# Mixture-of-experts tail on one core: another order of the expert programs, and five weight tiles subtracted on VectorE

## The chip, the core and the metric

One core of a Trainium2 chip runs the whole kernel. The metric is the device time of one execution in microseconds (us), from first to last instruction plus the little that lies around it. The median of three runs of the kernel before is 533.0 us (533.0 to 534.43). What can be told from no change with this kernel is about 0.3%, or 1.6 us.

The names of the engines are those of the profile: PE (TensorE matmuls; PEld is its weight load), DVE (VectorE), ACT (ScalarE), POOL (GpSimd), SP (SyncE, which only issues DMAs here). A "q" behind a name, as in PEldq, is the engine's sequencer: branches, register loads, semaphore waits.

## What is computed

Three stages, all in float32:

```python
x = attention(q, k, v)                 # 2 x 768 tokens, 8 heads of 64 -> x: 1536 x 512
x = elu(x @ w_in) @ w_out              # 512 -> 2048 -> 512
logits = x @ w_gate                    # 8 experts
e = argmax(logits, axis=1); gate_w = softmax(logits)[e]
# tokens go to their expert in order, at most capacity = 384 of them each
h = maximum(disp[e] @ w1[e], 0)        # 512 -> 1024
y = h @ w2[e]                          # 1024 -> 512
out[i] = gate_w[i] * y[token i]        # 0 for a token over the capacity
```

Everything that the change touches lies in the last stage, from the moment the tokens are routed.

## The kernel before

A float32 matmul is done as three passes of a faster type: each operand is split into a rounded half (`[:, 0]`, "hi") and the rest (`[:, 1]`, "lo"), and hi*hi, hi*lo and lo*hi are summed. So every 128x512 chunk of an expert's weights has to be *converted* before PE can use it: a cast from `rawq` (float32, fresh from DMA) to the hi half, mostly on ACT (L559), and a subtraction for the lo half (L560) on DVE or on POOL. That is `conv_expert(k, ms, pool, vec)`: chunks `ms` of expert `k`; those in `pool` have their subtraction on POOL, those in `vec` their cast on DVE. When a chunk is converted, its raw buffer is loaded again by SP. An expert has NCHUNK = 16 chunks, eight for w1 and eight for w2; experts of even and odd rank have tile sets `E0_*` and `E1_*`, and activation tiles `xbq0` and `xbq1`.

The experts are taken by falling number of tokens. The rank order is known only at run time, and so are the counts, so the program has branches (`tc.If`/`c.Else`, which end up as COMPARE_BRANCH on each of the five engines, after a TENSOR_LOAD of the count from `regs` in `count`, L1184). With the inputs of this case, the sorted counts are 880, 425, 168, 62, 1, 0, 0, 0. With blocks of 128 tokens and at most nj = 3 blocks for an expert, the work is:

- the first block of the largest expert (`Block`, tiles `bh0f`, `bh1f`), spread by hand over the end of the second stage and the routing of the last 384 tokens (L1069 to L1130). This part is one order written out by hand; `next(last)` runs a piece of the routing (`route`, L440 to L513) on DVE and PE, and `conv_expert(0, ...)` calls stand between the pieces;
- k = 0, the other two blocks of the same expert: `many_blocks(0, 2, ...)` (L692 `bh`, L681 `y`);
- k = 1 with three blocks, k = 2 with two blocks: `many_blocks`;
- k = 3 and k = 4 with one block: `one_block` (L618 `bh`, L626 transposes, L642 `y`). The last one has nothing to prefetch, and its names end in z (`bh_1z`).

While expert k computes, `more` converts the weights of expert k+1 in small portions and `ahead` transposes its gathered tokens (L582 `bt`); `finish` scales by the gate (L593 to L596) and scatters rows to `out` on POOL (L597).

Which code an expert runs is chosen by `blocks(k, cv, more_come)` with `choose(nb)`: is the count over 256? then three blocks; else over 128? then two; else one. Around it `experts(k, cv)` asks whether the next expert has tokens at all and puts the variant without prefetch into the Else branch, behind everything that the Then branch holds, all later experts included.

```python
                def choose(nb):
                    if k and nb == 1 and js[0] == 0:
                        body(1)
                        return
                    with tc.If(cv > js[nb - 1] * P) as c:
                        body(nb)
                    if nb > 1:
                        with c.Else():
                            choose(nb - 1)
            with tc.If(nxt > 0) as c:
                blocks(k, cv, True)
                experts(k + 1, nxt)
            with c.Else():
                blocks(k, cv, False)
```

So the program runs forward through code for three, two and one block of each expert, and jumps over what it does not need. Counted in PE's instruction list of the program (a matmul with its weight load counts as two), with these counts PE's way is: at the end of k=0 an unconditional jump of 170 instructions; end of k=1, one of 432; at k=2 a taken compare-branch of 363 (not over 256); end of k=2 an unconditional jump of 124; at k=3 taken compare-branches of 363 and 308 (not over 256, not over 128); after k=3 one of 4630 (no tokens in rank 5), then of 341 and 293 (not over 256, not over 128) to the block of k=4. The far jump is of 653 instructions on ACT, 605 on DVE, 268 on POOL and 446 on SP.

Of the kernel before, what the change touches and what calls it, by code (L numbers as in the profile page):

```python
# [20 lines left out]
P = 128  # L21
# [9 lines left out]
N = NB * S  # L31
# [10 lines left out]
NE = 8  # L42
# [4 lines left out]
GRP = 3  # L47


def build(tc, cap, qT, kT, vT, vP, wi, wo, wg, wgT, wx, out):  # L50
# [6 lines left out]
    with ctx:  # L57
# [488 lines left out]
        def raw_of(k, m):  # L546
            return RAW[m % NRAW] if k == 0 else RAW[((k - 1) * NCHUNK + m) % len(RAW)]

        def raw_load(k, ms):
            for m in ms:  # L550
                nc.sync.dma_start(raw_of(k, m), wx[ds(ereg[k], 1), :, m, :].rearrange("o p f -> p (o f)"))

        def conv_expert(k, ms, pool=(), vec=()):
            for m in ms:
                w, raw = EW[k][m], raw_of(k, m)
                if m in vec:
                    nc.vector.tensor_copy(w[:, 0], raw)
                else:
                    nc.scalar.copy(w[:, 0], raw)  # L559
                (nc.gpsimd if m in pool else nc.vector).tensor_tensor(w[:, 1], raw, w[:, 0].bitcast(F32), op=ALU.subtract)  # L560
                nxt = m + len(RAW)
                if nxt < NCHUNK:
                    raw_load(k, [nxt])
                elif 0 < k < NE - 1:
                    raw_load(k + 1, [nxt - NCHUNK])
# [8 lines left out]
        def gather(xg, gidx, n):  # L574
            nc.gpsimd.indirect_dma_start(
                out=xg, out_offset=None, in_=x2d[0:n, :],
                in_offset=bass.IndirectOffsetOnAxis(ap=gidx, axis=0))

        def load_xT(xb, col, xg, nm):
            pt = psm("bt" + nm, "TSO"[col // P])  # L580
            for c in range(NCC):
                nc.tensor.transpose(pt[:, c * P : (c + 1) * P], xg[:, c * P : (c + 1) * P], ident)  # L582
            ptv = pt.rearrange("p (c q) -> p c q", q=P)
            q = slice(col, col + P)
            nc.scalar.copy(xb[:, 0, :, q], ptv)
            nc.vector.tensor_tensor(xb[:, 1, :, q], ptv, xb[:, 0, :, q].bitcast(F32), op=ALU.subtract)
# [482 lines left out]
        next(last)  # L1069
        blk.first(0, 2)  # L1070
        blk.first(0, 3)
        conv_expert(0, range(11, 12), pool=range(NCHUNK))
        next(last)
        blk.turn(0, lo=False)
        blk.first(1, 0)
        conv_expert(0, range(12, NCHUNK), pool=range(NCHUNK))
        next(last)
        blk.turn_lo(0)
        blk.first(1, 1)
# [3 lines left out]
        blk.second(0)  # L1083
        blk.second(1)
        blk.turn(1, lo=False)
        next(last, None)
        blk.second(2)
        blk.second(3)
# [32 lines left out]

        GS = {0: slots(tf0.rearrange("p (j v) -> p j v", v=3), nj, "a") + (0,)}
        gathers(0, GRP)
        blk.turn_lo(1)
        cnt, key = count_key("1", NT)
        for f in range(4, 8):
            blk.second(f)
# [56 lines left out]
            return nc.values_load(regs[0:1, 1, k : k + 1], min_val=0, max_val=N,  # L1184
                                  skip_runtime_bounds_check_because="a count of tokens")

        def blocks(k, cv, more_come):

            jstart = 1 if k == 0 else 0
            gate, gidx, sidx, c0 = GS[k]  # L1190

            def fetch(nm, nb, pool):
                if not more_come:
                    return lambda n: None, lambda: None
                gathers(k + 1, nb)
                todo = list(range(NCHUNK))

                def more(n):
                    for m in todo[:n]:
                        conv_expert(k + 1, [m], pool, pool)  # L1200
                    del todo[:n]

                return more, lambda: ahead(k + 1, nb, nm)

            def only_fetch():
                more, ah = fetch(f"_{k}f", GRP, ())
                more(NCHUNK)
                ah()

            if k == 0 and nj == 1:  # L1210
                only_fetch()
            for j0 in range(jstart, nj, GRP):
                js = range(j0, min(nj, j0 + GRP))

                def body(nb):
                    sl = [c0 + j for j in js[:nb]]
                    nm = f"_{k}_{j0}_{nb}" + ("" if more_come else "z")
                    xb = XB[k % 2]
                    more, ah = lambda n: None, lambda: None
                    if j0 == jstart:  # L1220
                        more, ah = fetch(nm, GRP if k == 0 else nb, range(2, NCHUNK, 3) if nb == 1 else ())
                    else:
                        for i in range(nb):
                            gather(XG[i], gidx[:, sl[i] : sl[i] + 1], N)
                            load_xT(xb, i * P, XG[i], f"{i}" + nm)
                    args = (cols(gate, sl), cols(sidx, sl), nm, more, ah)
                    if nb == 1:
                        one_block(k, xb, *args)
                    else:
                        many_blocks(k, nb, xb, *args)  # L1230

                def choose(nb):
                    if k and nb == 1 and js[0] == 0:
                        body(1)
                        return
                    with tc.If(cv > js[nb - 1] * P) as c:
                        body(nb)
                    if nb > 1:
                        with c.Else():
                            choose(nb - 1)  # L1240
                    elif j0 == jstart and k == 0:
                        with c.Else():
                            only_fetch()

                choose(len(js))

        def experts(k, cv):

            if k + 1 == NE:
                blocks(k, cv, False)  # L1250
                return
            nxt = count(k + 1)
            with tc.If(nxt > 0) as c:
                blocks(k, cv, True)
                experts(k + 1, nxt)
            with c.Else():
                blocks(k, cv, False)

        experts(0, count(0))


_NAMES = ["qT", "kT", "vT", "vP", "wi", "wo", "wg", "wgT", "wx"]
# [35 lines left out]
```

## Time and profile before

| what | value |
| --- | --- |
| median of 3 runs | 533.0 us (533.0 to 534.43) |
| the profiled execution | 533.54 us, of which the span is 531.8 us |
| mean granted PE clock | 0.964 of full |
| PE busy | 482.4 us, 91% of the span |
| DVE, ACT, POOL busy | 335.8, 270.0, 202.1 us |
| chain that ended last, by engine | PE 65%, DVE 12%, DMA 8%, issue 7% |

"issue" is time in which an engine waited for nothing that the profile shows. Of the whole span PE is nearly always busy; the stretches in which it is not lie at the beginning, in the routing of the last tokens (374 to 393 us) and between the last experts (477 to 509 us).

### The profile page before, as it was taken

What the parts mean: (1) busy time and instruction counts of PE and PEld (TensorE: products, weight loads), DVE (VectorE), ACT (ScalarE), POOL (GpSimd) and SP (SyncE); (2) the same over time, 40 slices, a digit from 0 to 9 for tenths busy, and PEclk for the clock granted to TensorE, in tenths of its full rate; (3) what the DMA queues carried; (4) which work ended last, traced back from release to release, by engine and by line L of the source; (5) the groups of instructions that cost most, each with busy time, mean ns of one, the idle gap of its engine ahead of it and who ended that gap; (6) DMA issues with size and microseconds to landing.
All of it is one profiled execution on the core that took longest, in us unless ns stands there. A gap on an engine that the chain in (4) does not pass through costs nothing.

```text
span 531.8 us, 9284 instructions
## 1 busy us (share of the span) xinstructions
PE 482.4 (91%) x3052; PEld 415.0 (78%) x3052; DVE 335.8 (63%) x882; ACT 270.0 (51%) x688; POOL 202.1 (38%) x202
## 2 busy tenths in 40 slices
PE   6878888999999999999999999999889999896473
PEld 5666766878888889999999898888579898875362
DVE  4799999799888831111289888566767554563600
ACT  4656556865665456653333333337438654663310
POOL 4354756444334426862233232224650300302400
PEclk9998899999999999999999999999899999997868
DMA  8996574886666243465010100126349663764710
GB/s 235 299 244 187 167 214 122 265 253 216 181 208 178 80 127 92 120 252 164 0 61 0 60 0 2 60 65 221 112 137 337 215 219 109 219 203 130 221 35 6
DMA packets 45637, 80.01 MB, mean 150 GB/s; under 512 B 4604, under 2 KB 19196, under 8 KB 45552
## 3 DMA queue, kind: packets, MB, share of 16 engines
q1 hardware_dynamic: 43792, 73.83, 45.0%
q0 software_dynamic: 1760, 5.19, 3.2%
q8 instruction: 36, 0.59, 0.5%
q14 instruction: 49, 0.40, 0.3%
HBM read 65.29 MB, written 13.11 MB: 147 GB/s over the span
## 4 chain that ended last, share of the span: by engine, by line
PE 65%; DVE 12%; DMA 8%; issue 7%; another core or an unknown queue 3%; ACT 2%; POOL 1%; POOLq 0%; SPq 0%; DVEq 0%
PE acc L373 23%; PE h L340 22%; PE bh L692 6%; PE y L681 5%; DMA out<-ys,sidx 5%; DMA vt<-vT 3%; PE S L231 2%; PE O L279 2%; DVE t1i L319 2%; DVE t1o L322 1%; DVE t1i L322 1%; DVE st L258 1%; ACT sc L252 1%; PE T L267 1%
## 5 line engine op out<-in xcount | busy, mean ns | idle before, releaser
L340 PE MATMUL h<-xT,Wi 128*128 128x384 f32 x768 | 150.5, 345 | 8.2 <-DVE e L351 6.6
L340 PEld LDWEIGHTS h<-xT,Wi 128*128 128x128 f32 x768 | 138.3, 192 | 15.8 <-DVE e L351 8.7
L373 PE MATMUL acc<-Wo,g 128*128 128x512 f32 x576 | 146.8, 398 | 1.7 <-POOL Wo L329 1.0
L360 POOL TENSOR_TENSOR g<-e,g 128x384 fp32r<-128x384 f32 x63 | 77.2, 1225 | 123.4 <-ACT g L356 108.7
L373 PEld LDWEIGHTS acc<-Wo,g 128*128 128x128 f32 x576 | 105.4, 188 | 23.6 <-POOL Wo L329 1.3
L351 DVE SCALAR_TENSOR_TENSOR e<-e,h 128x384 f32<-128x384 f32 x64 | 35.3, 552 | 75.6 <-ACT e L347 75.6
L346 ACT ACTIVATE e<-h 128x384 f32<-128x384 f32 x64 | 31.5, 493 | 58.9 <-PE h L340 56.8
L260 POOL TENSOR_TENSOR sc<-sc,st 128x360 f32<-128x360 f32 x32 | 31.3, 979 | 67.2 <-DVE st L259 54.7
L560 DVE TENSOR_TENSOR E<-rawq,E 128x512 fp32r<-128x512 f32 x65 | 43.5, 713 | 11.9 <-ACT E L559 10.7
L252 ACT ACTIVATE sc<-sc,st 128x120 f32<-128x120 f32 x96 | 36.7, 384 | 26.4 <-DVE st L245 26.3
L356 ACT CAST g<-e 128x384 fp32r<-128x384 f32 x64 | 32.8, 512 | 33.2 <-DVE e L351 33.2
L692 PE MATMUL bh<-xbq,E 128*128 128x256 f32 (+1 forms) x288 | 43.3, 302 | 2.6 <-ACT ys L593 1.9
L692 PEld LDWEIGHTS bh<-xbq,E 128*128 128x128 f32 x288 | 41.2, 188 | 4.7 <-issue 1.7
L559 ACT CAST E<-rawq 128x512 fp32r<-128x512 f32 x75 | 42.5, 617 | 1.3 <-issue 0.7
L681 PE MATMUL y<-E,g 128*128 128x512 f32 x168 | 41.7, 393 | 0.0
L435 DVE CUSTOM_DVE_ANT_0 dot<-a,wgb 128x512 f32<-128x512 f32 x48 | 40.0, 888 | 0.0
L681 PEld LDWEIGHTS y<-E,g 128*128 128x128 f32 x168 | 30.6, 188 | 5.7
L347 ACT ACTIVATE e<-e 128x384 f32<-128x384 f32 x64 | 33.6, 526 | 2.0
L271 ACT COPY pT<-T 120x384 f32<-120x384 f32 x32 | 15.3, 478 | 37.0 <-PE T L267 36.7
L245 DVE CUSTOM_DVE_ANT_0 sc<-S,masks 128x120 f32<-128x120 f32 x96 | 22.0, 276 | 10.0 <-PE S L231 8.1
L231 PE MATMUL S<-kw,qt 64*64 64x120 f32 x384 | 27.1, 274 | 0.4 <-DVE st L245 0.3
L700 DVE TENSOR_TENSOR g<-e,g 128x256 fp32r<-128x256 f32 (+1 forms) x24 | 11.3, 471 | 25.4 <-ACT g L699 25.3
(216 smaller groups left out, 644.9 us busy)
## 6 DMA issues: line engine op xcount, KB each, us to landing
rawq<-wx SPq DMA_DIRECT2D x88, 256.0 KB, 3.8
rawi<-wi SPq DMA_DIRECT2D x16, 512.0 KB, 4.8
rawo<-wo SPq DMA_DIRECT2D x16, 512.0 KB, 4.7
vw<-vP SPq DMA_DIRECT2D x16, 288.0 KB, 6.7
kt<-kT SPq DMA_DIRECT2D x8, 400.0 KB, 5.8
qt<-qT SPq DMA_DIRECT2D x16, 192.0 KB, 4.9
vt<-vT SPq DMA_DIRECT2D x8, 384.0 KB
out<-xg SPq DMA_DIRECT2D x12, 256.0 KB, 3.0
```

Source lines behind the costliest of these rows:

```text
L231: nc.tensor.matmul(ps[r, gi * KEYS : (gi + 1) * KEYS], lhsT=QT[p][r, (g0 + gi) * QB : (g0 + gi + 1) * QB], rhs=KW[p][r, g0 + gi, :], start ...
L252: nc.scalar.activation(out=sc[:, gi], in_=sc[:, gi], func=AF.Exp, bias=st[:, 0, gi : gi + 1], scale=-1.0, accum_out=st[:, 1, gi : gi + 1])
L340: nc.tensor.matmul(HP[t, f][:, 0:TT], lhsT=w[:, s, c * P : (c + 1) * P], rhs=xT[t][:, xs, c, :], start=c == 0 and n == 0, stop=c == NCC - ...
L347: nc.scalar.activation(out=e, in_=e, func=AF.Relu, bias=1.0, scale=-1.0)
L351: nc.vector.scalar_tensor_tensor(out=e, in0=e, scalar=-1.0, in1=h[:, 0:TT], op0=ALU.mult, op1=ALU.max)
L360: eng.tensor_tensor(g[:, 1], EP.pop((t, f)), g[:, 0].bitcast(F32), op=ALU.subtract)
L373: nc.tensor.matmul(accp[tb], lhsT=g[:, s, tb * P : (tb + 1) * P], rhs=w[:, ws], start=f % FPG == 0 and n == 0, stop=f % FPG == FPG - 1 and ...
L435: nc.vector.tensor_tensor_reduce(out=junk, in0=x2[t * BPT + tb], in1=WGB[e // 2][:, e % 2], scale=1.0, scalar=0.0, op0=ALU.mult, op1=ALU.a ...
L559: nc.scalar.copy(w[:, 0], raw)
L560: (nc.gpsimd if m in pool else nc.vector).tensor_tensor(w[:, 1], raw, w[:, 0].bitcast(F32), op=ALU.subtract)
L681: nc.tensor.matmul(ys[b], lhsT=g[:, s, b * P : (b + 1) * P], rhs=w[:, ws], start=f == 0 and n == 0, stop=f == 7 and n == 2)
L692: nc.tensor.matmul(h[:, 0:nt], lhsT=EW[k][half * NCC + c][:, ws, fc * P : (fc + 1) * P], rhs=xb[:, s, c, 0:nt], start=n == 0, stop=n == 3 ...
```

## The change

Two parts.

1. `conv_expert` is split into `conv_hi` and `conv_lo`. For the chunks 11 to 15 of the largest expert the subtraction moves from POOL to DVE. The one of chunk 11 stays in its place, that of 12 comes just ahead of the last `next(last, None)`, that of 13 behind `gathers(0, GRP)`, those of 14 and 15 behind `blk.turn_lo(1)`. The five casts stay on ACT where they were.
2. `blocks`, `choose` and `experts` give way to `large` and `small`. `large(k)` holds the code for two and three blocks of expert k and, inside its Then branch, `large(k+1)`; if the count is not over 128 it jumps to a copy of `small(k)`, which stands behind that. `small(k)` is a straight chain: the block of k with prefetch, the same without prefetch, and then `small(k+1)`. k = 0 has its own `first_expert`.

```diff
+        def conv_hi(k, ms, vec=()):
+            for m in ms:
+                (nc.vector.tensor_copy if m in vec else nc.scalar.copy)(EW[k][m][:, 0], raw_of(k, m))
+
         def conv_expert(k, ms, pool=(), vec=()):
             for m in ms:
+                conv_hi(k, [m], vec)
+                conv_lo(k, [m], pool)
+
+        def conv_lo(k, ms, pool=()):
+            for m in ms:
                 w, raw = EW[k][m], raw_of(k, m)
...
-        conv_expert(0, range(11, 12), pool=range(NCHUNK))
+        conv_expert(0, range(11, 12))
         next(last)
         blk.turn(0, lo=False)
         blk.first(1, 0)
-        conv_expert(0, range(12, NCHUNK), pool=range(NCHUNK))
+        conv_hi(0, range(12, NCHUNK))
         next(last)
...
         blk.turn(1, lo=False)
+        conv_lo(0, range(12, 13))
         next(last, None)
...
         gathers(0, GRP)
+        conv_lo(0, range(13, 14))
         blk.turn_lo(1)
+        conv_lo(0, range(14, NCHUNK))
         cnt, key = count_key("1", NT)
...
-        def blocks(k, cv, more_come):
...
-                def choose(nb):
...
-        def experts(k, cv):
...
+        def single(k, j, nxt):
+
+            nm = f"_{k}_{j}" + ("z" if nxt is None else "")
+            more, ah = fetch(NE if nxt is None else nxt, nm, GRP if k == 0 else 1, range(2, NCHUNK, 3))
+            one_block(k, XB[k % 2], *slots_of(k, [j]), nm, more, ah)
...
+        def small(k, cv):
+
+            with tc.If(cv > 0):
+                if k + 1 == NE:
+                    single(k, 0, None)
+                    return
+                nxt = count(k + 1)
+                with tc.If(nxt > 0) as c:
+                    single(k, 0, k + 1)
+                with c.Else():
+                    single(k, 0, None)
+                small(k + 1, nxt)
+
+        def large(k, cv):
...
+            with tc.If(cv > P) as c:
+                nxt = count(k + 1) if k + 1 < NE else None
+                if nj == 2:
+                    several(k, range(2))
+                else:
+                    with tc.If(cv > 2 * P) as d:
+                        several(k, range(GRP))
+                        others(k, cv, GRP)
+                    with d.Else():
+                        several(k, range(2))
+                if nxt is not None:
+                    large(k + 1, nxt)
+            with c.Else():
+                small(k, cv)
...
-        experts(0, count(0))
+        cv0, cv1 = count(0), count(1)
+        first_expert(cv0, min(GRP, nj - 1))
+        large(1, cv1)
```

What moves is best seen in the engines' instruction lists. First DVE at the end of the routing, before (`tab` is the table of rows that the routing fills, `gidxa` and `sidxa` the row numbers of the largest expert's blocks, `hTf1` the turned half of the first block):

```order
L499 TENSOR_TENSOR B3_2_4358<-orv3_4334,J3_4336 128x72
L513 TENSOR_TENSOR tab_119<-tp3_4377,tab_119 128x72
L1101 TENSOR_TENSOR tw0_4397<-tab_119,sel0_3994 128x72
L1105 TENSOR_REDUCE tf0_4399<-tw0_4397 128x9
L529 TENSOR_SCALAR gidxa_4406<-tf0_4399 128x3
L531 TENSOR_TENSOR gatea_4408<-tf0_4399 128x3
L533 TENSOR_SCALAR pada_4410<-tf0_4399,padid_102 128x3
L534 TENSOR_TENSOR pada_4410<-pada_4410,tf0_4399 128x3
L536 TENSOR_SCALAR sidxa_4413<-pada_4410 128x3
L635 TENSOR_TENSOR hTf1_4199<-ht1f_4371,hTf1_4199 128x512
```

and with the change:

```order
L565 TENSOR_TENSOR E0_12_4031<-rawq0_4007,E0_12_4031 128x512
L513 TENSOR_TENSOR tab_119<-tp3_4374,tab_119 128x72
L1107 TENSOR_TENSOR tw0_4394<-tab_119,sel0_3994 128x72
L1111 TENSOR_REDUCE tf0_4396<-tw0_4394 128x9
L529 TENSOR_SCALAR gidxa_4403<-tf0_4396 128x3
L531 TENSOR_TENSOR gatea_4405<-tf0_4396 128x3
L533 TENSOR_SCALAR pada_4407<-tf0_4396,padid_102 128x3
L534 TENSOR_TENSOR pada_4407<-pada_4407,tf0_4396 128x3
L536 TENSOR_SCALAR sidxa_4410<-pada_4407 128x3
L565 TENSOR_TENSOR E0_13_4032<-rawq1_4008,E0_13_4032 128x512
L640 TENSOR_TENSOR hTf1_4199<-ht1f_4367,hTf1_4199 128x512
L565 TENSOR_TENSOR E0_14_4033<-rawq2_4009,E0_14_4033 128x512
```

One subtraction of 128x512 stands ahead of the row numbers, one ahead of `hTf1`, two behind it (the second of them, E0_15, is the next row); chunk 11 stands some 30 rows earlier, ahead of the copy of the logits.

Second, PE where the program leaves one expert and chooses the code of the next, here from the one-block code of k=2 to the three-block code of k=3, before:

```order
L642 MATMUL y_2_0_1_6416<-E0_15_4034,hT1_2_0_1_6362 128x512 x3
L1236 UNCONDITIONAL_BRANCH
L1184 TENSOR_LOAD regs_4454
L1253 COMPARE_AND_BRANCH
L1236 COMPARE_AND_BRANCH
L692 MATMUL bh0_3_0_3_6506<-xbq1_4405,E1_0_4487 128x384 [waits Activation_49]
```

and with the change, the end of the two-block code of k=2:

```order
L686 MATMUL y1_2_0_2_5958<-E0_15_4034,g7_2_0_2_6192 128x512 x3
L1262 UNCONDITIONAL_BRANCH
L1257 COMPARE_AND_BRANCH
L1192 TENSOR_LOAD regs_4454
L1262 COMPARE_AND_BRANCH
L697 MATMUL bh0_3_0_3_6239<-xbq1_4402,E1_0_4487 128x384 x2
```

The one-block code no longer stands between them; the row L1257 is the test "over 128" of k=3, whose taken branch goes to the copy of `small(3)`. Third, the end of k=3 in that chain, with the change:

```order
L647 MATMUL y_3_0_10642<-E1_15_4502,hT1_3_0_10588 128x512 x3
L1246 UNCONDITIONAL_BRANCH
L623 MATMUL bh0_3_0z_10720<-E1_0_4487,xbq1_4402 128x512 x3
...
L647 MATMUL y_3_0z_10755<-E1_15_4502,hT1_3_0z_10719 128x512 x3
L1246 UNCONDITIONAL_BRANCH
L1241 COMPARE_AND_BRANCH
L1192 TENSOR_LOAD regs_4454
L1246 COMPARE_AND_BRANCH
L623 MATMUL bh0_4_0_10812<-E0_0_4019,xbq0_4401 128x512 [waits Activation_49]
```

The block of k=3 with prefetch jumps over the block without, as long as an expert's block, and lands on the L1241 row, the test of k=4.

Counted as before, PE's way with the change is: end of k=0, unconditional 170; end of k=1, unconditional 308; at k=2 a taken compare-branch of 362; nothing at its end; at k=3 a taken compare-branch of 5220 into `small(3)`; end of k=3, unconditional 114; at k=4 a taken compare-branch of 123 to the block without prefetch. The far jump is of 736 instructions on ACT, 815 on DVE, 394 on POOL and 726 on SP, and it lies ahead of k=3 instead of behind it.

## Rows read from the trace of the kernel before

**Rows 1.** PE's idle time by what it waited for, 400 to 532 us: total, times, longest.

```profile
PE bh_1z L618 <- issue: 10.9, 1, 10.9
PE bh L618 <- issue: 5.4, 1, 5.4
PE bh L692 <- ACT ys L593: 1.9, 2, 1.4
```

**Rows 2.** Windows by stage: length, busy PE, PEld, DVE, ACT, POOL; granted clock; DMA share, GB/s.

```profile
452.70:477.80 25.10, 23.79 (x152) 21.24 (x152) 15.24 (x27) 16.54 (x37) 4.09 (x5) 1.00 0.69 220
477.80:483.20 5.40, 0.07 (x1) 0.10 (x1) 2.12 (x4) 1.58 (x3) 3.14 (x4) 0.72 0.46 134
483.20:497.60 14.40, 14.35 (x60) 11.36 (x60) 6.49 (x11) 6.04 (x11) 3.28 (x3) 0.87 0.46 142
497.60:508.40 10.80, 0.00 (x0) 0.03 (x1) 4.38 (x7) 2.12 (x4) 4.12 (x3) 0.64 0.75 216
508.40:523.40 15.00, 14.96 (x56) 11.68 (x56) 1.38 (x2) 2.37 (x4) 0.00 (x0) 0.80 0.02 4
```

**Rows 3.** Branches of line 1236, 448 to 454 us: ns min/median/max, first and last start.

```profile
L1236 PEldq COMPARE_BRANCH  x3: 73/310/4376, 448.4 to 453.7; - x3
```

**Rows 4.** Branches of line 1236, 470 to 485 us.

```profile
L1236 PEldq COMPARE_BRANCH  x3: 190/3487/3696, 474.9 to 479.3; - x3
L1236 ACTq COMPARE_BRANCH  x3: 38/50/50, 477.8 to 478.5; - x3
...
L1236 POOLq COMPARE_BRANCH  x3: 38/50/50, 479.9 to 480.6; - x3
```

**Rows 5.** Branches of line 1253, 490 to 510 us.

```profile
L1253 PEldq COMPARE_BRANCH  x1: 4188/4188/4188, 494.8 to 494.8; - x1
...
L1253 POOLq COMPARE_BRANCH  x1: 45/45/45, 503.5 to 503.5; - x1
```

**Rows 6.** Branches of line 1236, 499 to 504 us.

```profile
L1236 PEldq COMPARE_BRANCH  x1: 5015/5015/5015, 499.1 to 499.1; - x1
```

**Rows 7.** Branches of line 1236, 504 to 508.5 us (the first row takes one from group 6 again).

```profile
L1236 PEldq COMPARE_BRANCH  x2: 4100/4558/5015, 499.1 to 504.1; - x2
L1236 POOLq COMPARE_BRANCH  x2: 45/48/50, 507.4 to 507.6; - x2
```

**Rows 8.** Register loads of the counts, line 1184, whole run.

```profile
L1184 PEldq TENSOR_LOAD <-regs x6: 298/310/497, 391.6 to 494.4; - x6
```

**Rows 9.** DMA queues of the whole run (the page): packets, MB, share of 16 engines.

```profile
q8 instruction: 36, 0.59, 0.5%
```

**Rows 10.** DMA issues, 440 to 532 us: count, median us from issue to landing.

```profile
xgq<-x2d,gidx POOLq DMA_INDIRECT x3, 4.2
```

**Rows 11.** Windows with the granted clock, columns as in group 2.

```profile
378.00:380.50 2.50, 0.03 (x1) 0.00 (x0) 2.40 (x5) 0.15 (x1) 2.50 (x3) 1.00 0.01 3
381.20:384.50 3.30, 3.30 (x9) 2.12 (x8) 3.27 (x21) 0.82 (x2) 0.45 (x1) 0.50 0.00 0
508.30:512.00 3.70, 3.60 (x9) 2.85 (x10) 0.00 (x0) 0.00 (x0) 0.00 (x0) 0.50 0.04 9
514.30:516.00 1.70, 1.70 (x10) 1.40 (x10) 0.00 (x0) 0.34 (x1) 0.00 (x0) 1.00 0.00 0
```

**Rows 12.** DVE's groups by line, 376.8 to 381.8 us: busy us, mean ns, idle before.

```profile
L458 DVE TENSOR_TENSOR L<-L,sm 128x24 f32<-128x24 f32 x1 | 1.3, 1314 | 0.0
L452 DVE TENSOR_TENSOR cand<-cand,wt_e 128x24 f32<-128x24 f32 x1 | 1.2, 1183 | 0.0
L450 DVE TENSOR_TENSOR cand<-L,sm 128x24 f32<-128x24 f32 x1 | 1.1, 1078 | 0.0
L455 DVE TENSOR_TENSOR oh<-wt_e,sm 128x24 bf16<-128x24 f32 x1 | 1.0, 977 | 0.0
```

**Rows 13.** Line 450 in the whole run: the four rounds of the routing.

```profile
L450 DVE TENSOR_TENSOR cand<-L,sm x4: 182/185/1078, 293.3 to 376.9; 128x24 f32<-128x24 f32 x4
```

**Rows 14.** Subtractions of the lo half on DVE, whole run (the page).

```profile
L560 DVE TENSOR_TENSOR E<-rawq,E 128x512 fp32r<-128x512 f32 x65 | 43.5, 713 | 11.9 <-ACT E L559 10.7
```

More of the change, by code (lines that the diff above doesn't have):

```diff
@@ L551, in raw_load @@
                 nc.sync.dma_start(raw_of(k, m), wx[ds(ereg[k], 1), :, m, :].rearrange("o p f -> p (o f)"))
+        def conv_hi(k, ms, vec=()):
+            for m in ms:
+                (nc.vector.tensor_copy if m in vec else nc.scalar.copy)(EW[k][m][:, 0], raw_of(k, m))
         def conv_expert(k, ms, pool=(), vec=()):
             for m in ms:
+                conv_hi(k, [m], vec)
+                conv_lo(k, [m], pool)
+        def conv_lo(k, ms, pool=()):
+            for m in ms:
                 w, raw = EW[k][m], raw_of(k, m)
[L556 to L559, printed above, removed]
                 (nc.gpsimd if m in pool else nc.vector).tensor_tensor(w[:, 1], raw, w[:, 0].bitcast(F32), op=ALU.subtract)
@@ L1185, in count @@
                                   skip_runtime_bounds_check_because="a count of tokens")
-        def blocks(k, cv, more_come):
[L1189 to L1210, printed above, removed]
-                only_fetch()
[L1212 to L1230, printed above, removed]
-                def choose(nb):
[L1233 to L1245, printed above, removed]
@@ L1247, in experts, with fetch, more, slots_of @@
-        def experts(k, cv):
-            if k + 1 == NE:
-                blocks(k, cv, False)
+        def fetch(k, nm, nb, pool):
+            if k >= NE:
+                return lambda n: None, lambda: None
+            gathers(k, nb)
+            todo = list(range(NCHUNK))
+            def more(n):
+                for m in todo[:n]:
+                    conv_expert(k, [m], pool, pool)
+                del todo[:n]
+            return more, lambda: ahead(k, nb, nm)
+        def slots_of(k, js):
+            gate, _, sidx, c0 = GS[k]
+            sl = [c0 + j for j in js]
+            return cols(gate, sl), cols(sidx, sl)
@@ new lines, in single, with several @@
+        def single(k, j, nxt):
+            nm = f"_{k}_{j}" + ("z" if nxt is None else "")
+            more, ah = fetch(NE if nxt is None else nxt, nm, GRP if k == 0 else 1, range(2, NCHUNK, 3))
+            one_block(k, XB[k % 2], *slots_of(k, [j]), nm, more, ah)
+        def several(k, js):
+            nb = len(js)
+            if nb == 1:
+                single(k, js[0], k + 1)
+                return
+            nm = f"_{k}_{js[0]}_{nb}"
+            more, ah = fetch(k + 1, nm, GRP if k == 0 else nb, ())
+            many_blocks(k, nb, XB[k % 2], *slots_of(k, js), nm, more, ah)
@@ new lines, in others @@
+        def others(k, cv, j0):
+            _, gidx, _, c0 = GS[k]
+            for j in range(j0, nj):
+                with tc.If(cv > j * P):
+                    gather(XG[0], gidx[:, c0 + j : c0 + j + 1], N)
+                    load_xT(XB[k % 2], 0, XG[0], f"_{k}_{j}o")
+                    one_block(k, XB[k % 2], *slots_of(k, [j]), f"_{k}_{j}o", lambda n: None, lambda: None)
+        def small(k, cv):
+            with tc.If(cv > 0):
+                if k + 1 == NE:
+                    single(k, 0, None)
+                    return
+                nxt = count(k + 1)
[4 more added lines that the diff above has]
+                small(k + 1, nxt)
@@ new lines, in large @@
+        def large(k, cv):
+            if nj == 1:
+                small(k, cv)
+                return
+            with tc.If(cv > P) as c:
[11 more added lines that the diff above has]
+            with c.Else():
+                small(k, cv)
@@ L1251, in experts, with only_fetch, first_expert @@
+        def only_fetch():
+            more, ah = fetch(1, "_0f", GRP, ())
+            more(NCHUNK)
+            ah()
+        def first_expert(cv, nb):
+            if nb == 0:
+                only_fetch()
                 return
[L1252 to L1255, printed above, removed]
+            with tc.If(cv > nb * P) as c:
+                several(0, range(1, nb + 1))
+                if nb == GRP:
+                    others(0, cv, nb + 1)
@@ L1256, in experts @@
             with c.Else():
-                blocks(k, cv, False)
-        experts(0, count(0))
+                first_expert(cv, nb - 1)
+        cv0, cv1 = count(0), count(1)
+        first_expert(cv0, min(GRP, nj - 1))
+        large(1, cv1)
 _NAMES = ["qT", "kT", "vT", "vP", "wi", "wo", "wg", "wgT", "wx"]
```

## Prediction

> **What bounds the kernel now.** I read PE's waits first, then windows by stage, then the branch records, then the granted clock. The waits show where PE, busy for 91% of the span, stands still late in the run: 10.9 us ahead of the last block (`bh_1z`), 5.4 us ahead of the block of k=3, and 1.4 us once ahead of a `bh` of line 692; the first two are put down to "issue", that is to nothing the profile shows [rows 1]. The windows say that these are pure gaps: PE does nothing from 477.8 to 483.2 us and from 497.6 to 508.4 us [rows 2]. The branch records fill both. PE's sequencer comes to its branches before its matmuls are done: at 474.9 where the stage ends at 477.8, at 494.8 where it ends at 497.6, a lead of 2.8 us each time [rows 2, 4, 5]. Then it sits in compare-branches: 3.5 and 3.7 us one after the other up to 483 us [rows 4], and 4.2, 5.0 and 4.1 us up to 508.2 us [rows 5 to 7]. Ahead of k=2 there is one more of 4.4 us [rows 3]. Which of PE's branches these are follows from the way that is counted out ahead: every taken compare-branch, of 293 to 4630 instructions, took 3.5 to 5.0 us, while the shortest record at 474.9, the unconditional jump of 124, took 0.19 us and the one of 432 instructions some 0.31 us [rows 3, 4]. An instruction queue of PE moves 0.59 MB in 36 packets, 16 KB each [rows 9], so instructions are fetched while the program runs. The stalls are jumps to code that is not there yet. The gaps are the stalls less the lead: 3.5 + 3.7 + some register load - 2.8 is near 5.4; 4.2 + 5.0 + 4.1 - 2.8 is near 10.8.
>
> **The gap from k=3 to k=4.** Today 10.8 us [rows 2]. With the change the stretch from k=3's last matmul to k=4's first holds an unconditional jump of 114, two compare-branches and a register load, and the taken one is a hop of 123 instructions. By the rows: 0.19 for a jump like that [rows 4], 0.31 for the load [rows 8], 0.07 for a branch not taken [rows 3], and for the hop the value of the short unconditional jump, 0.2 to 0.3. That is 0.9 us, well inside the lead of 2.8. No trace shows a taken compare-branch of PE that short; the bounds are 0.2 (that jump) and 5.0 [rows 6]. I take the low end, since ACT's short taken branches, three at 477.8 to 478.5, lie within 0.7 us [rows 4], so a taken branch as such is not slow. Gain 10.7 us.
>
> **The clock after it.** [...] PE had stood still for 10.8 us before. Without the gap it goes on at full clock: between 508.4 and a point from 512.0 to 514.3 it ran at half, 3.6 to 5.9 us, half of which is 1.8 to 2.9. I take 2.7.
>
> **The gap from k=2 to k=3.** Today 5.4 us. The change drops two near stalls (3.5 and 3.7) and puts one far jump of 5220 instructions there. Its price is read from the far jump of 4630 in the trace, 4.2 us [rows 5]; bounds 3.5 and 5.0 [rows 4, 6]. Behind it come one load and two branches, 0.5, and 0.2 to the first matmul; the lead of 2.8 goes off: 2.1 us are left. Gain 3.3, from 2.5 to 4.0. Whether the clock falls here is open: it was 1.00 behind the 1.4 us gap ahead of k=2, and 0.50 from 381.2 on after PE had nearly nothing to do from 378.0 to 380.5 [rows 1, 2, 11]. 2.1 lies nearer to 2.5, so I leave the loss of k=3 in place; up to 1.9 more if it goes.
>
> The other engines make their far jump here too now. In the trace it costs POOL 3.9 us (503.5 to 507.4) [rows 5, 7], and I take that for all four; they stall beside PE, as each of them leaves k=2. PE needs ACT first for `hs`, 12 matmuls into the block, about 3 us; ACT comes to its branches at 477.8 with PE's end [rows 4], is free 4 us later, has two casts to do, and would be wanted 2.1 + 3 = 5.1 us after that end: late by 0 to 1. POOL leaves k=2 at 479.9 [rows 4], 2.1 us after PE's end; with the stall and a gather that takes 4.2 to land [rows 10], and about 1 us of load and issue, the tokens of k=4 are there 11.2 us after that end. PE transposes them ahead of the last nine of the block's 60 matmuls, some 10 us into it, 12 us after that end. Cover is there, but thin: 0 to 2 us in all, I take 0.3. DVE and ACT, busy for 6.5 and 6.0 of the 14.4 us of k=3 [rows 2], have room to catch up. The conversions of k=4 that now lie in the gap (DVE 4.4 us busy, ACT 2.1, POOL 4.1 [rows 2]) will run beside k=4 itself. They are chunks 12 to 15, which PE reads only in the last third of the block, 9 us on. I cost that at nothing; if that cover fails, it is rival C.
>
> [...]
>
> **The gap from k=1 to k=2.** 1.4 us, put down to ACT's `ys` [rows 1], but the branch of 4.4 us ends at 453.7 and so holds PE as well [rows 3]. The taken branch there stays (362 for 363), the branch behind it goes. Bounds: nothing, and all of 1.4. The jump behind the end of k=1 is now 308 instead of 432, which brings the start of the taken one no nearer, but its target lies 126 instructions less far along; if it costs 3.5 as at 475.7 [rows 4] instead of 4.4, 0.9 is gained. With the branch, 1.0.
>
> **The routing.** Four small DVE operations, 128x24 elements each, take 0.98 to 1.31 us there [rows 12], 4.55 together, while the same line takes 0.18 in the other rounds [rows 13]. During them POOL runs the subtractions that the change takes from it. Without POOL they cost 4 x 0.18, a gain of up to 3.8 us on DVE, on which PE waits in that stretch. Against it DVE does five subtractions of 0.71 [rows 14], 3.6 us. Those of chunks 11 and 12 lie ahead of the row numbers, 1.4 us on the chain; the first falls partly into DVE's wait for the logits. Those of 13 to 15, 2.1 us, lie behind the row numbers, so the gather starts without them, but ahead of the counts that PE's first branch needs. So from +0.5 (contention stays in part, DVE full) to -2.7 (3.8 less 1.1). I take -1.0.
>
> **The end.** POOL passes one branch more and jumps further at the very end, 0 to 0.6; I take 0.3.
>
> **Sum.** Against 533.54, the profiled run: -10.7 - 2.7 - 3.3 + 0.3 - 1.0 - 1.0 + 0.3 = -18.1, so 515.4. That run is 0.5 above the median of 533.0, so I forecast 515.0.
>
> **Rivals.**
>
> A. A taken compare-branch of PE costs 3.5 to 5.0 however short it is. For it: all six that the trace shows did. Against it: none of them was short, and on ACT short ones are quick. Then k=4 waits 4.1 + 0.7 - 2.8 = 2.0 us and perhaps starts at half clock again (2.7): 517 to 519.7. 0.15.
>
> B. The branches are not what PE waits for, and the gaps stay. [...] Against it stand the records of 3.5 to 5.0 us, which fill the gaps to 0.3 us. Only the routing's 1 us would be left: 532.0 to 533.5. 0.04.
>
> C. The gap goes, but k=3 or k=4 wait for engines that landed late: POOL's gather, or the conversions of chunks 12 to 15, 4.4 us of DVE. The time is 2 to 7 us above mine: 517 to 522. 0.08.
>
> D. Slower: the five engines' far stalls add up, each engine waiting for the next at its first instruction: 4.2 on PE [rows 5] and 3.9 on each of the other four is 20 us, at both transitions, 40 against 16.2 today: 533.5 + 24 - 2 for the earlier stretches = 555. It decides from about 9 us at each. Against it: today's far jump had all five in it, and PE's gap was just PE's own three stalls. 0.03.
>
> **How the numbers follow.** My case has 0.70, from 511 (all upper gains but not the clock of k=3) to 517.5; A and C reach to 520 for most of their chance. The range is 511 to 520, with the rest of C, B and D left out, and the low tail. Faster by over 0.3% (1.6 us, about what a measurement can tell) takes my case, A, C and a part of B: 0.94; the same 0.03, slower 0.03.
>
> **What would show it.** Right: the stage of k=4 follows that of k=3 with no gap, at clock 1.00; one compare-branch of PE of about 4.2 us ahead of k=3 with a gap near 2 us; the L450 to L458 group at 0.2 us each. Wrong: a stall ahead of k=4 (A), the gaps as they were (B), PE waiting for DMA or DVE within the two blocks (C), gaps of over 9 us (D).

## The result, and the profile after

The changed kernel takes 515.72 us in the median of 4 runs (513.84 to 517.51) against 533.71 (533.0 to 535.68): a ratio of 0.9657, with a 95% interval of 0.9611 to 0.9702. That is 18.0 us less; 18.1 less was forecast, and 515.0 us.

The profiled run of the changed kernel is the slowest of the four, 517.51 us with a span of 515.6. First its windows by stage: length, busy PE, PEld, DVE, ACT and POOL, granted clock, DMA share, GB/s. They are k=2, the gap behind it, k=3, k=4, and the end.

```profile
453.20:476.50 23.30, 23.17 (x150) 21.05 (x151) 15.25 (x27) 16.44 (x36) 3.87 (x4) 1.00 0.71 234
476.50:479.10 2.60, 0.65 (x3) 0.19 (x1) 0.48 (x1) 0.47 (x1) 1.67 (x2) 1.00 0.28 102
479.10:493.90 14.80, 14.17 (x60) 11.17 (x60) 8.30 (x13) 7.19 (x13) 5.54 (x5) 0.88 0.54 167
493.90:505.70 11.80, 11.80 (x57) 9.55 (x56) 6.17 (x10) 4.40 (x8) 4.18 (x3) 1.00 0.63 199
505.70:515.60 9.90, 0.62 (x3) 0.18 (x1) 0.48 (x1) 0.47 (x1) 1.01 (x1) 0.73 0.08 14
```

Set beside [rows 2]: the idle 10.8 us are gone, k=4 follows k=3 and is busy in every microsecond, at a clock of 1.00 and in 11.8 us where it was 15.0 at 0.80. DVE, ACT and POOL now do in it (6.2, 4.4 and 4.2 us) what they did in the gap. The gap ahead of k=3 is 2.0 to 2.6 us where it was 5.4, and k=3 still starts at a lower clock (0.88 in the mean of the stage). PE's waits from 385 us on (total, times, longest) say the same; they answer to [rows 1]:

```profile
PE bh L623 <- issue: 2.0, 1, 2.0
PE bh L697 <- ACT ysf L601: 1.4, 1, 1.4
PE yf L647 <- DVE hTf L640: 1.0, 1, 1.0
PE bh L697 <- ACT ys L598: 0.6, 1, 0.6
PE y L647 <- DVE hT L640: 0.6, 1, 0.6
```

The branches, line by line of the new code: ahead of k=2 (448 to 451 us), ahead of k=3 (470 to 480 us), ahead of k=4 (490 to 493 us), as ns min/median/max and first and last start. They answer to [rows 3 to 7].

```profile
L1262 PEldq COMPARE_BRANCH  x2: 954/1966/2977, 448.8 to 450.3; - x2
```

```profile
L1257 PEldq COMPARE_BRANCH  x1: 3808/3808/3808, 474.3 to 474.3; - x1
L1257 ACTq COMPARE_BRANCH  x1: 50/50/50, 477.2 to 477.2; - x1
L1257 DVEq COMPARE_BRANCH  x1: 74/74/74, 477.7 to 477.7; - x1
L1257 POOLq COMPARE_BRANCH  x1: 50/50/50, 478.9 to 478.9; - x1
```

```profile
L1246 PEldq COMPARE_BRANCH  x2: 225/259/293, 491.1 to 492.0; - x2
```

PE's far jump into the chain costs 3.8 us, and the hop ahead of k=4 0.23 us: the first two rows that the prediction asked for. The routing's small operation and DVE's subtractions, to be set beside [rows 13, 14], are

```profile
L450 DVE TENSOR_TENSOR cand<-L,sm x4: 182/185/186, 296.1 to 379.9; 128x24 f32<-128x24 f32 x4
```

```profile
L565 DVE TENSOR_TENSOR E<-rawq,E 128x512 fp32r<-128x512 f32 x70 | 47.7, 722 | 10.9 <-ACT E L555 9.9
```

All four rounds of line 450 are now alike at 0.18 us, and DVE has 70 subtractions where it had 65.

To see where the 18 us come from, I took from each trace the start of the same eight weight loads of PE, so that each column is one stage with the gap behind it. The routing is counted from the first weight load of `bh1f`, the end from PE's last weight load to the end of the span. The first column is the 200th weight load of the kernel, in the attention, which no edit touches. All in us:

| kernel | 200th load at | routing | k=0 | k=1 | k=2 | k=3 | k=4 | end |
| --- | --- | --- | --- | --- | --- | --- | --- | --- |
| before | 26.1 | 17.7 | 24.8 | 36.2 | 29.2 | 25.3 | 14.4 | 9.1 |
| before, second profile | 29.1 | 17.9 | 24.8 | 36.3 | 29.2 | 23.2 | 13.3 | 9.1 |
| before, third profile | 27.5 | 18.2 | 24.8 | 36.4 | 29.4 | 23.6 | 13.5 | 8.9 |
| changed | 28.4 | 14.7 | 25.3 | 35.2 | 25.8 | 14.8 | 11.8 | 9.9 |
| changed, second profile | 29.1 | 14.7 | 25.3 | 35.6 | 25.8 | 12.5 | 12.8 | 9.9 |
| subtractions alone | 28.4 | 14.8 | 26.7 | 36.2 | 29.3 | 26.1 | 14.5 | 9.2 |
| order of experts alone | 27.6 | 18.3 | 24.8 | 35.0 | 25.1 | 14.5 | 11.8 | 9.5 |
| hop of 203 | 28.4 | 14.7 | 25.3 | 34.6 | 26.5 | 12.9 | 12.6 | 9.3 |
| hop of 203, shifted | 29.9 | 14.7 | 26.8 | 37.5 | 25.2 | 15.0 | 11.7 | 9.5 |
| no far jump | 26.6 | 14.7 | 25.3 | 34.5 | 23.6 | 13.4 | 12.2 | 9.9 |
| chunk 11 on POOL | 28.3 | 14.2 | 25.7 | 35.4 | 25.1 | 12.9 | 12.2 | 9.7 |
| counts first | 28.2 | 14.2 | 25.8 | 34.5 | 24.8 | 13.3 | 12.4 | 11.0 |

The two profiled runs differ by 16.2 us of span and not 18 to 19 because the changed one was 2.3 us later in the attention already. That is scatter: the kernel before, profiled three times, came to that point at 26.1, 29.1 and 27.5 us. The stages scatter too, k=3 and k=4 above all. By the means of the three profiles before and the two after, the columns from the routing on differ by -3.2, +0.5, -0.9, -3.5, -10.4, -1.4 and +0.9, together -18.0.

### The profile page after: what moved, and what is told of

Read it like the earlier page. It is cut to its first block, busy times and chain, and to the rows that moved or that the text cites. A ratio compares the mean times of both kernels' runs of the same rounds, so it can differ in the third digit from the quotient of the medians.

```text
span 515.6 us, 9263 instructions
## 1 busy us (share of the span) xinstructions
PE 481.3 (93%) x3052; PEld 414.0 (80%) x3052; DVE 335.3 (65%) x887; ACT 270.3 (52%) x688; POOL 196.5 (38%) x197
## 5 line engine op out<-in xcount | busy, mean ns | idle before, releaser
L565 DVE TENSOR_TENSOR E<-rawq,E 128x512 fp32r<-128x512 f32 x70 | 47.7, 722 | 10.9 <-ACT E L555 9.9
L271 ACT COPY pT<-T 120x384 f32<-120x384 f32 x32 | 15.3, 479 | 36.7 <-PE T L267 36.4
L231 PE MATMUL S<-kw,qt 64*64 64x120 f32 x384 | 28.9, 287 | 0.0
L231 PEld LDWEIGHTS S<-kw,qt 64*64 64x64 f32 x384 | 21.3, 143 | 6.1 <-issue 3.9
```

What stands on the lines that cost most here:

```text
L231: nc.tensor.matmul(ps[r, gi * KEYS : (gi + 1) * KEYS], lhsT=QT[p][r, (g0 + gi) * QB : (g0 + gi + 1) * QB], rhs=KW[p][r, g0 + gi, :], start ...
```

## The experiments

### Each part alone

The kernel before with the five subtractions moved, and the experts as they were:

```diff
-        conv_expert(0, range(11, 12), pool=range(NCHUNK))
+        conv_expert(0, range(11, 12))
-        conv_expert(0, range(12, NCHUNK), pool=range(NCHUNK))
+        conv_hi(0, range(12, NCHUNK))
...
+        conv_lo(0, range(12, 13))
...
+        conv_lo(0, range(13, 14))
...
+        conv_lo(0, range(14, NCHUNK))
```

> The kernel before with the first part of the change alone: the five subtractions on DVE, the expert programs as they were. Forecast's theory: 1.0 us less than the kernel before (0.5 more to 2.7 less), the four DVE operations of lines 450 to 458 at 0.18 us each, the two gaps of 5.4 and 10.8 us unchanged. Rival, from the trace of the changed kernel, where the stretch from the second logits matmuls to the start of k=0 was 3.0 us shorter: 2.5 to 3 us less. If the five subtractions were the cost that DVE's chain cannot hide: 0 to 2 us more.

Measured: 532.23 us (530.76 to 536.66), a ratio of 0.9949 (0.9932 to 0.9965) to the kernel before, that is 2.7 us less (1.9 to 3.6). One of the five runs, the profiled one, took 536.66 us, longer than any run of the kernel before in that comparison. The rival from the trace named the amount, not the forecast's 1.0, whose range ended at 2.7. Its rows: line 450 in all rounds, now at 0.18 us, and PE's two long waits (from 385 us on), which are as in the kernel before.

```profile
L450 DVE TENSOR_TENSOR cand<-L,sm x4: 182/182/186, 296.3 to 379.8; 128x24 f32<-128x24 f32 x4
```

```profile
PE bh_1z L623 <- issue: 11.2, 1, 11.2
PE bh L623 <- issue: 5.5, 1, 5.5
```

The profiled run lost some of it again in k=0, 26.7 us where 24.8 were; the windows show why in the part on the clock below.

The other half: the changed kernel with all five subtractions back on POOL.

```diff
-        conv_expert(0, range(11, 12))
+        conv_expert(0, range(11, 12), pool=range(NCHUNK))
-        conv_hi(0, range(12, NCHUNK))
+        conv_expert(0, range(12, NCHUNK), pool=range(NCHUNK))
...
-        conv_lo(0, range(12, 13))
...
-        conv_lo(0, range(13, 14))
...
-        conv_lo(0, range(14, NCHUNK))
```

> The changed kernel with the five subtractions put back on POOL where they were: the new order of expert programs alone. Forecast's theory: 17.1 us less than the kernel before (the sum without the routing's 1.0), no gap ahead of k=4, about 2 us ahead of k=3, the four DVE operations of lines 450 to 458 at about 1.1 us each again. If the two parts are independent, this and the run with the first part alone add up to the whole change. Rival: the parts help each other, and this one gives less than 15.

Measured: 519.62 us (517.8 to 520.37), 0.9727 (0.9711 to 0.9744), 14.6 us less than the kernel before in that comparison (13.7 to 15.4). The two parts together, 2.7 + 14.6 = 17.3, are near the 18.0 of the whole; they add up within their intervals. The forecast's 17.1 was 2.5 too much. That this one gives less than 15 is just what the rival said, but the table shows no help between the parts: its stages from k=1 to k=4 are those of the changed kernel. The slowed operation is back:

```profile
L450 DVE TENSOR_TENSOR cand<-L,sm x4: 183/185/1078, 294.7 to 378.4; 128x24 f32<-128x24 f32 x4
```

1.08 us in the last round with POOL's subtractions beside it, 0.18 without, twice each way: it is POOL's work that slows DVE's small operations there. How it does so is not shown; when, the trace of the kernel before tells. POOL's four subtractions run there end to end, and each of DVE's four slow operations, which read two tiles, ends 0.04 us behind one of them (at 378.01, 379.23, 380.46 and 381.69 us). A reduction between them, which reads one tile, takes 0.18 us as ever. POOL's row and that reduction:

```profile
376.67 4.98 POOL L560 TENSOR_TENSOR E<-rawq,E 128x512 fp32r<-128x512 f32 x4 [0.56 <-ACT E L559]
```

```profile
L453 DVE TENSOR_REDUCE sm<-cand 128x3 f32<-128x24 f32 x1 | 0.2, 178 | 0.0
```

### What a taken branch costs

The forecast took the stalls to be jumps to code that is not there yet, and the hop ahead of k=4 to be cheap; rival A took a taken compare-branch to be dear at any length. The 0.23 us of the changed kernel speak against A, but a price by length (0.2 at 123 instructions, 3.5 at 293) would fit as well. So the hop was made 203 long, by 40 pairs of PE instructions that are never executed, and in a second kernel shifted by 200 instructions with the same length.

```diff
                         others(k, cv, GRP)
+                        if k == 2:
+                            busy(20)
...
                     single(k, 0, k + 1)
+                    if k == 4:
+                        busy(40)
```

> The changed kernel with PE instructions that are never executed put into two branches: 40 into the three-block code of k=2 and 80 into the block of k=4 with prefetch. [...] Theory that the length of a taken branch sets its price (123 gave 0.23, 293 and more gave 3 to 5): somewhere between, 1 to 3 us. [...]

The second kernel has `busy(120)` in place of `busy(20)`.

> As the run with the hop of 203, with 240 instead of 40 dead PE instructions at k=2, so that the code of k=4 is shifted by 200. [...] Theory of length: the same price as in the run without the shift. [...]

The rows of the two, the branches ahead of k=4 first (the hop is the larger of the two) and those ahead of k=2 next (the taken one is the larger). Hop of 203, 515.92 us in one run:

```profile
L1246 PEldq COMPARE_BRANCH  x2: 192/262/331, 489.3 to 490.0; - x2
```

```profile
L1264 PEldq COMPARE_BRANCH  x2: 301/1673/3045, 448.7 to 449.6; - x2
```

Shifted, 521.86 us in one run:

```profile
L1246 PEldq COMPARE_BRANCH  x2: 292/1897/3502, 494.3 to 495.1; - x2
```

```profile
L1264 PEldq COMPARE_BRANCH  x2: 1403/3076/4748, 451.9 to 453.9; - x2
```

The same hop of 203 instructions costs 0.33 us in one place and 3.5 us in the other, where a price by length would have been the same in both. Length does not set the price; where the code lies does, as the two kernels differ only in the 200 dead instructions ahead of it. At k=2, where the length changed with the place, the taken branch took 3.0 us at 402 and 4.7 us at 602, and in the kernel before the taken branches of 363 at k=2 and at k=3 took 4.4 and 3.5 us [rows 3, 4]. That a shift of 200 would make the hop dear was my estimate; what makes a place dear is not shown beyond these prices and the packets below.

The fetches themselves are in the trace. Queue q8, of the kind "instruction", moves packets of 16 KB [rows 9]: in the kernel before, 19 of them up to 390 us, ahead of PE's first branch, for 4873 of PE's recorded instructions. Each of the eleven branches of PE of over 2 us in the profiles of the kernel before (seven) and of the changed one (four) has at least one of them in it. In the shifted kernel one runs from 496.3 to 497.2 us, inside the hop of 495.1 to 498.6; around the near hop, from 489.2 to 491.0 us, only q1 moved anything. The queues in these two windows (494 to 499 us in the shifted kernel, then the other):

```profile
q8 instruction: 1, 0.02, 1.2%
```

```profile
q1 hardware_dynamic: 278, 0.50, 89.0%
```

PE's gap ahead of k=4 in the shifted kernel was this wait:

```profile
PE bh_0z L623 <- ACT E L555: 1.5, 1, 1.5
```

It is put down to a conversion on ACT, but that is only what else ended late; the branch began at 495.1 and ended at 498.6, and the matmul came at 498.8.

### The far jump

The changed kernel still has one far jump, ahead of k=3. Without the code for more blocks from rank 3 on, which these counts never run, it is gone:

```diff
-            if nj == 1:
+            if nj == 1 or k == 3:
                 small(k, cv)
                 return
```

> The changed kernel without the code for two and three blocks of the experts of rank 3 and later (it leaves out what those would need; with these counts nothing of it is executed), so that k=3 follows k=2 in the program on every engine and the far jump is gone. Forecast's theory: PE's gap of 2 to 2.6 us ahead of k=3 goes, as one compare-branch of 3.8 us does; DVE, ACT and POOL are no longer late in k=3, so PE's wait of 1.2 us there for the lo half of hT goes too, and the half clock at the start of k=3 (about 2.5 us long, 1.2 lost). Together 4 to 5 us less than the changed kernel. Rival: only the branch itself, 2 to 2.6 us, since PE would wait for the conversions anyway.

Measured: 512.39 us (510.76 to 514.46), 0.9606 (0.9567 to 0.9645). Against the changed kernel beside it in the same comparison (515.98, below) 3.6 us less. That lies between the two theories (4 to 5, and 2 to 2.6), and the scatter of both kernels is as large as what separates them. By the table 2.2 of it lie in the stage of k=2 with its gap, the rival's amount; k=3 gives 1.4 against the first profile of the changed kernel and nothing against the second. The rows are clearer: the branch ahead of k=3, PE's waits from 470 us on, and the first 2 us of k=3.

```profile
L1241 PEldq COMPARE_BRANCH  x1: 65/65/65, 472.8 to 472.8; - x1
```

```profile
PE y L647 <- DVE hT L640: 0.7, 1, 0.7
PE ht_0z L631 <- ACT hs_0z L626: 0.2, 1, 0.2
```

```profile
475.30:477.30 2.00, 2.00 (x10) 1.64 (x9) 0.95 (x2) 1.61 (x3) 1.31 (x2) 1.00 0.24 96
```

The gap is gone, and the clock is at 1.00. But PE waits for the lo half of `hT` in k=3 as before, 0.7 us by this view and 1.35 between two weight loads (1.17 in the changed kernel). So one part of the expectation fell: without the far jump DVE begins its subtractions 1.6 us behind PE's first weight load of k=3 (3.2 in the changed kernel), and PE waits all the same. In the kernel before there was no such wait, and DVE had converted the first chunks of k=4 while PE stood in the gap; without the gap DVE has four subtractions and a cast ahead of the lo half of `hT`. And one of the four is slow. Here and then in the changed kernel, the last two of them, and POOL beside them:

```profile
479.59 2.58 DVE L565 TENSOR_TENSOR E<-rawq,E 128x512 fp32r<-128x512 f32 x2 [0.93 <-ACT E L555]
479.71 1.30 POOL L565 TENSOR_TENSOR E<-rawq,E 128x512 fp32r<-128x512 f32 x1
```

```profile
484.89 1.30 POOL L565 TENSOR_TENSOR E<-rawq,E 128x512 fp32r<-128x512 f32 x1
484.94 2.41 DVE L565 TENSOR_TENSOR E<-rawq,E 128x512 fp32r<-128x512 f32 x2 [0.97 <-ACT E L555]
```

Two subtractions on DVE take 1.29 us elsewhere. The first of each pair took 1.98 and 1.80 us where 0.69 is usual, and ended 0.56 us behind POOL's: it is the collision of the routing again. Less the 1.3 and 1.1 us, `hT` would have come before PE asked for it. Late engines can do it as well: in the two kernels with the hop of 203 no subtraction ahead of `hT` is slowed, DVE begins 3.5 and 3.8 us into the block, and 0.9 and 1.2 us lie between the same two loads (0.23 where nothing waits).

How late they land can still be read, in the changed kernel, from the next branch of each engine (first start):

```profile
L1241 ACTq COMPARE_BRANCH  x4: 34/39/50, 480.1 to 507.0; - x4
L1241 DVEq COMPARE_BRANCH  x4: 43/52/56, 481.7 to 508.0; - x4
L1241 POOLq COMPARE_BRANCH  x4: 34/41/50, 482.1 to 509.3; - x4
```

Against 477.2, 477.7 and 478.9 above, the far jump cost ACT 2.9 us, DVE 4.0 and POOL 3.2; the forecast had 3.9 for each, read from POOL alone. In the kernel before, ACT's and DVE's were 3.0 (499.6 to 502.6 us) and 3.6 (500.3 to 503.9). The jumps run at the same time, which is what rival D denied.

### Three small edits, the counts, and a control

```diff
-        conv_expert(0, range(11, 12))
+        conv_expert(0, range(11, 12), pool=range(NCHUNK))
...
-            more(3)
+            more(1)
             blk.first(1, 0)
             blk.first(1, 1)
             blk.turn(0)
-            more(1)
+            more(3)
...
-        cv0, cv1 = count(0), count(1)
-        first_expert(cv0, min(GRP, nj - 1))
-        large(1, cv1)
+        first_expert(count(0), min(GRP, nj - 1))
+        large(1, count(1))
```

> The changed kernel with three small edits: the subtraction of chunk 11 on POOL again (in the kernel before it ran there ahead of the four slowed DVE operations, so it should not slow them), the one-block code converting one chunk ahead of the first transposes and three behind them instead of the other way round, and the count of k=1 loaded only behind k=0. By the traces: 0.35 us less ahead of the copy of the logits, up to 1.2 less in k=3 where PE waits for DVE, 0.3 less ahead of k=0: 1 to 2 us less than the changed kernel. Rival: chunk 11 on POOL pushes no DVE operation but another engine's path stays the bound, and nothing of it is seen in the time, which scatters by some 2 us from run to run.

> The changed kernel as it is, again, as the control for the three runs beside it: 514 to 517.5 us. In its profile the first 200 weight loads of PE, which the change does not touch, ended at 26.1 us in the profile of the kernel before and at 28.4 in that of the changed one; if that is scatter from run to run and not the change, this run may show anything from 26 to 30.

Measured: 514.28 us (513.27 to 515.95), 0.9639 (0.961 to 0.9667), and the control 515.98 us (512.41 to 517.38), 0.9663 (0.9628 to 0.9698). The intervals overlap by most of their length: 1.7 us in the medians, as expected, but not shown. Its trace says that each edit did its own part and a later wait took some of it: the routing is 0.5 us shorter, k=0 is 0.4 longer. PE's wait of 1.4 us for `ysf` is gone, with two waits for DVE in its place that were not there or were smaller:

```profile
PE bh L697 <- DVE tabs L1179: 1.0, 1, 1.0
PE bh L697 <- DVE xbq L591: 0.6, 1, 0.6
...
PE y L647 <- DVE hT L640: 0.3, 1, 0.3
```

PE's wait for `hT` in k=3 is down to 0.3: its lo half now comes ahead of the slowed subtraction (1.84 us), which still meets POOL's. Behind k=0's start DVE is what PE waits for.

On top of that, all counts read behind k=0:

```diff
+        cvs = [None] + [count(k) for k in range(1, NE)]
+        large(1, cvs[1])
...
-                nxt = count(k + 1)
+                nxt = cvs[k + 1]
```

> As the run before, and all counts from rank 1 on loaded together behind k=0, so that no register load stands between the branches later. By the records of the changed kernel (0.3 to 0.6 us a load on PE): 0.4 less ahead of k=2, 0.6 less ahead of k=3; the seven loads behind k=0, 2.2 us, lie inside the 2.8 us that PE's sequencer is ahead. 2 to 3 us less than the changed kernel. Rival: the loads delay DVE (0.4 us each) or POOL (0.5) at the start of k=1 and PE waits for them there: up to 2 us more.

Measured: 514.71 us (512.18 to 517.24), 0.9646 (0.9614 to 0.9679): no better. The gap ahead of k=3 was the shortest of those with the far jump, 0.9 us in the waits where the changed kernel has 2.0, and k=1 and k=2 are among the shortest too; the end of the run is 1.1 us longer. The trace shows SyncE last there: its sequencer stands still for 4.8 us behind its last branch and for 2.6 us once more, and its closing drain ends 1.2 us behind POOL's, where in the changed kernel POOL's is last. What held it the second time is not shown.

```profile
PE bh L623 <- issue: 0.9, 1, 0.9
```

Last, the kernel before twice more, for the scatter of the start.

> The kernel before as it is, for a second profile. If the 2.3 us by which the first 200 weight loads of PE ended earlier in the first profile of the kernel before (26.1 us against 26.6 to 29.9 in eight other kernels' profiles) is scatter from run to run, this one may show 26 to 30. If it were something that all the changed programs have and the kernel before has not, it would show 26 again. The stages behind the routing as in the first profile: gaps of 5.4 and 10.8 us.

> The same once more, as one profile tells little about scatter.

Measured: 534.07 and 533.5 us, one run each; the 200th load at 29.1 and 27.5 us. It is scatter.

## Why the prediction was right

**The gap from k=3 to k=4, -10.7.** Right. The stage of k=3 with its gap fell from 25.3 to 14.8 us, 10.5 less, in which the forecast's 0.3 of lateness is contained (-10.4 together). The hop costs 0.23 us. The low end of the bounds was the right one. The reason given for it, that ACT's taken branches are quick, is a weak one: ACT's far jump costs 2.9 us. What speaks for it is the near hop of 203, 0.33 us with no packet of q8 beside it; shifted, with one in it, the same hop takes 3.5.

**The clock behind it, -2.7.** Right in kind: with no gap ahead of it k=4 runs at 1.00, where it had started at 0.50 [rows 11]. The size was read from the one profile of three in which k=4 is longest. In the first pair k=4 went from 14.4 to 11.8 us, 2.6 less. But the kernel before has 13.3 and 13.5 in the other two, and the changed kernel 12.8 at full clock in its second, with PE waiting 0.8 us for `hs`; by the means it is 1.4 less.

**The gap from k=2 to k=3, -3.3.** Right: the stage of k=2 with its gap went from 29.2 to 25.8, 3.4 less. The far jump took 3.8 us where 4.2 was taken, the register load behind it up to 0.6 where 0.3 was.

**Late engines in k=3, +0.3.** Mis-sized and put down to the wrong cause: 1.2 us lay between two loads of PE that waited for DVE, and 1.35 without a far jump. What the forecast lacks is POOL's own subtraction of k=4 beside DVE's, which in the changed kernel cost DVE 1.1 us just ahead of `hT`; in its second profile POOL's began only when `hT` was under way, and 0.4 us lay between these loads. POOL's gather, which I had feared, held nothing up.

**The gap from k=1 to k=2, -1.0.** Right, 36.2 to 35.2, but by two errors that cancel. The taken branch is 3.0 us where it was 4.4, so it gave 1.4 and not 0.9. The unconditional jump at the end of k=1, which took 0.3 us at a length of 432, took 1.0 at 308 (and 0.3 to 1.5 in the other profiles); the forecast had no term for it.

**The routing, -1.0.** Mis-sized by two thirds: 17.7 to 14.7 us, 3.0 less, of which k=0 gives back 0.5. The step that failed is the 1.4 us for chunks 11 and 12 and part of the 2.1 for the others, which I laid on the chain. By the traces chunk 11 cost 0.35 us and chunk 12 nothing, as it fits into the 0.5 us for which DVE had waited for PE's `tp`. What DVE lost by the slow operations is 3.8 us; 3.0 of it came back although DVE does five subtractions more.

**The end, +0.3.** It was 0.8, by the reason given: behind PE's last weight load POOL's last branch comes 0.2 us later, and its jump takes 3.4 us where it took 2.8.

The sum by the first pair of profiles: -10.5 - 2.6 - 3.4 - 1.0 - 3.0 + 0.5 + 0.8 = -19.2; by the means of all five it is -18.0. That 18.0 us came out against 18.1 is in part luck. Each part alone shows it: the new order gave 14.6 us (13.7 to 15.4) where the terms of the forecast give 17.1, and the subtractions 2.7 (1.9 to 3.6) where they give 1.0. By the means, the clock of k=4 and the end account for 1.9 of the 2.5 that the new order gave less than forecast; the routing gave it back.

The rivals: A fell with the 0.23 us, B with the gap that went with its branches, D because the far stalls lay beside each other. C was half there: PE does wait for DVE in k=3, for 1 us and not for 2 to 7, and in the changed kernel because POOL held DVE up and not because DVE landed late.

## What to carry to other kernels

Where a wait is put down to nothing ("issue"), look at the sequencer's own records: on PE the stalls here were compare-branches of 3 to 5 us with a packet of q8 in them, and their price went with the place of the code, not with the length (0.33 and 3.5 us for the same 203 instructions). On ACT, DVE and POOL the record of the far jump is short (50 to 74 ns), and the 2.9 to 4.0 us lie between it and the engine's next record. Lay out the code that is likely to run in the order in which it runs, on each engine; the engine sits still only for what the stall exceeds its sequencer's lead (2.8 us here). A subtraction on an idle engine is not free if it slows short operations on the path of another: four operations of 0.18 us had become 4.6 together. With the experts closed up, the same happened to a subtraction in k=3 (1.80 us where 0.69 is usual).

## What the runs showed of the hardware that was not expected

The clock behind a short stop is not the same from run to run. In the changed kernel PE stands for some 2 us ahead of k=3, in both profiles. Windows of the first profile, then of the second:

```profile
479.20:481.00 1.80, 1.80 (x5) 1.47 (x6) 0.00 (x0) 0.14 (x1) 0.26 (x1) 0.60 0.25 68
481.00:483.00 2.00, 2.00 (x6) 1.52 (x6) 0.65 (x2) 1.00 (x2) 0.00 (x0) 0.50 0.02 6
```

```profile
479.00:481.00 2.00, 2.00 (x9) 1.65 (x10) 0.00 (x0) 0.52 (x1) 0.36 (x1) 1.00 0.23 66
```

The first fell to 0.50, the second stayed at 1.00; k=3 took 14.8 and 12.5 us, of which some 0.7 is the longer wait for DVE in the first. The same at the start of k=0, where PE had stood for a little over a microsecond: the run with the subtractions alone fell, the changed kernel did not.

```profile
394.00:396.00 2.00, 1.91 (x11) 1.77 (x10) 0.87 (x6) 0.64 (x2) 0.68 (x1) 0.63 0.58 177
396.00:398.00 2.00, 2.00 (x12) 2.00 (x12) 0.42 (x1) 0.26 (x2) 1.39 (x3) 0.52 0.99 325
```

```profile
394.00:396.00 2.00, 1.79 (x15) 1.77 (x15) 0.96 (x7) 0.80 (x2) 0.96 (x1) 1.00 0.55 168
396.00:398.00 2.00, 2.00 (x18) 1.95 (x17) 0.77 (x2) 0.80 (x2) 1.40 (x2) 1.00 0.91 320
```

That costs 1.4 us in k=0 (26.7 against 25.3), and it is a good part of the 2 to 5 us by which runs of one kernel differ. Stops of 5 and 10 us were followed by a clock of 0.50 in all three profiles of the kernel before. And an unconditional jump is not cheap as such: at the end of k=1 the same one took between 0.3 and 1.5 us. The packets of q8 go with it: where it took 0.4 to 1.5 us (six profiles), it ended 1.4 to 1.5 us after a packet of 16 KB had landed; where it took 0.30 (two), the packet had landed 1.3 and 1.7 us before it began.
